# Re-timing the opening of a fused attention and feed-forward kernel, and recutting its last output tile

## The chip, the cores and the metric

One core of one Trainium2 chip. The metric is the device time of one execution in microseconds (us). The kernel before was given as 327.79 us, the median of three executions (327.70 to 327.82). "Span" is the time from the first to the last instruction in a trace; an execution's time is its span plus about 1.8 us.

Engine names as the profile has them: PE is TensorE's products, PEld its weight loads, DVE is VectorE, ACT is ScalarE, POOL is GpSimd, SP is SyncE; a "q" behind a name is the engine's instruction queue, for example where it issues a DMA.

## The reference

Two stages in a row (shortened). Linear attention with cosine weights, for 8 batches, 8 heads, 576 positions and head dimension 64:

```python
def phi(x, c, s):
    r = np.maximum(x, 0.0)
    return np.concatenate([r * c, r * s], axis=-1)
q_p, k_p = phi(q, cos_w, sin_w), phi(k, cos_w, sin_w)
kv  = np.einsum('bhsf,bhsd->bhfd', k_p, v)
z   = np.sum(k_p, axis=2)
num = np.einsum('bhsf,bhfd->bhsd', q_p, kv)
den = np.einsum('bhsf,bhf->bhs', q_p, z)[..., None] + 1e-06
out = num / den
```

then, on 4608 tokens of width 512, RMS normalisation and a gated feed-forward layer of width 1536:

```python
xn = x / np.sqrt(np.mean(x * x, axis=-1, keepdims=True) + 1e-06) * rms_g
g = xn @ w_gate
return (g / (1 + np.exp(-g))) * (xn @ w_val) @ w_out
```

## The kernel before

After an opening of about 31 us the kernel is a long row of products with 512 columns: for each of nine blocks of tokens, 12 steps of gate and value products (`gval_mm`), then output products. Every engine's order is fixed by the program. The opening is where batch 0 is loaded, its attention computed, and the first half of block 0's feed-forward run in small pieces. The parts that the argument touches (cuts marked `...`; V, A, G are VectorE, ScalarE, GpSimd):

```python
load_kv("k", 0, *LOW); load_kv("k", 0, *HIGH)
load_q_tokens(0, 0, 2)
first_v = load_kv("v", 0, *LOW)             # head pairs 0 and 1
load_kv("v", 0, 2, 3); load_kv("v", 0, 3, 4)  # pair 2, pair 3
...
filler(12, idle)          # products on zeros, to get TensorE's clock granted
paced(7, 1); paced(0, 3)
nc.tensor.matmul(psG[0][:, :], lhsT=ones[:, :], rhs=g_row[:, :], start=True, stop=True)
paced(5, 3)
...                       # weight slices are released by first_v
v_cast(A, 0, 0, 1); v_cast(V, 0, 1, 2); v_cast(A, 0, 2, 3)
q_tr_evac(V, 0, 0, psV[0][:, :])
kvz_mm(0, low_banks, LOW)                   # phi(k)' [v, 1], pairs 0 and 1
kvz_copy(A, 0, 0, low_banks[0], LOW); kvz_copy(A, 0, 1, low_banks[1], LOW)
v_cast(V, 0, 3, 4)
kvz_mm(0, high_banks, (2, 3))               # pair 2
filler(1, idle)
nd_half(0, 0, 0, psV[0]); nd_post_half(0, 0, 0, psV[0])   # first half of x tile 0
kvz_mm(0, high_banks, (3, 4))               # pair 3
...
nd_half(0, 0, 1, psO[1]); nd_post_half(0, 0, 1, psO[1])
...
x_sq(0, 0)                                  # ACT square and sum, POOL power
...
x_norm(0, 0)                                # DVE
x_tr_pe(0, 0, psG[1][:, :]); x_tr_evac(V, 0, 0, psG[1][:, :])   # x transposed by TensorE
...
open_ffn(2, (4, 5), 0, 256, parts=(0,))     # gate products of steps 4 and 5
x_tr_pe(0, 2, psA[:, 0, :])                 # transposes of x tile 2
...
# batch 1: k waits for the fourth pair of weight slices
d = load_kv("k", 1)
tc.add_manual_dep(d.ins, weight_dmas[7].ins.name, SYNC_DEP, reason="after the weights")
...
# last output tile, in two halves of 256 columns
for half, bank in ((0, psC[1]), (1, psG[0])):
    c = slice(256 * half, 256 * half + 256)
    for n in range(NNT):
        nc.tensor.matmul(bank[:, 0:256], lhsT=hTs[8][:, n, 3 * P : 4 * P], rhs=wo[:, n, c], ...)
    copy(A, osb[:, c], bank[:, 0:256])
    for i in range(2):
        r0 = (6 + i) * S + 512
        (nc.sync if i == 0 else A).dma_start(
            out=out[r0 : r0 + 64, c], in_=osb[64 * i : 64 * i + 64, c])
```

## Time and profile before

| reading | value | view |
|---|---|---|
| time of the profiled execution, its span | 328.54, 326.73 us | times, page |
| PE busy | 98% of the span | page |
| landing of v: first two pairs, last pair | 10.58, 12.18 us | chain, queue |
| x_norm of tile 0 starts | 16.63 us | chain |
| first full-width gate product (step 6) | 31.43 us | PE timeline |
| end of the last product to end of span | 3.72 us | PE timeline |

The profiled execution took 328.54 us, 0.75 more than the three timed ones.

From the page of the kernel before: the span, each engine's busy time, and the shares of the chain of waits.

```profile
span 326.7 us, 6408 instructions
...
PE 318.9 (98%) x2427; PEld 161.3 (49%) x2427; DVE 186.3 (57%) x412; ACT 175.7 (54%) x365; POOL 31.9 (10%) x67
...
PE 91%; DMA 3%; DVE 2%; ACT 2%; issue 1%; SPq 0%; POOL 0%; DVEq 0%
```

PE is the limit almost everywhere, so a change elsewhere can pay only in PE's few holes or at the two ends.

The chain of waits of the kernel before in the opening (start us, length us, what):

```profile
2.27 8.31 DMA rv<-in_v_dram
...
14.29 0.17 DVE rec L344
...
15.22 0.73 ACT scr L374 x2
...
16.63 0.76 DVE xn L386
17.39 0.05 issue
17.44 0.40 PE psG L411 x4
```

The whole opening hangs on one DMA: v lands at 2.27 + 8.31 = 10.58 us.

VectorE's timeline of the kernel before between the casts of v and the two half normalisations (start us, length us, engine, line, operation, out<-in, shapes, count, and in brackets the idle time before it and what ended it):

```profile
12.20 0.76 DVE L264 CAST vvm<-rv 128x576 bf16<-128x576 f32 x1 [0.24 <-DMA rv<-in_v_dram]
13.06 0.16 DVE L344 TENSOR_SCALAR rec<-psV 128x4 f32<-128x4 f32 x1
...
14.29 0.16 DVE L344 TENSOR_SCALAR rec<-psO 128x4 f32<-128x4 f32 x1 [0.40 <-PE psO L325]
```

The weight loads' timeline of the kernel before, at the transposes of x (L411) and one more hole:

```profile
17.43 0.23 PEld L411 LDWEIGHTS <-xn 128*128 128x128 bf16 x4 [1.20 <-DVE xn L386]
...
19.46 0.23 PEld L411 LDWEIGHTS <-xn 128*128 128x128 bf16 x4 [0.21 <-DVE xn L386]
...
24.45 0.23 PEld L411 LDWEIGHTS <-xn 128*128 128x128 bf16 x4 [0.42 <-DVE xn L386]
...
27.05 0.21 PEld L561 LDWEIGHTS <-wg 128*128 128x128 bf16 x3 [0.26 <-issue]
```

These brackets are the holes that the second part of the change aims at.

ScalarE's timeline of the kernel before in the tail:

```profile
321.73 0.37 ACT L262 COPY osb<-psC 128x256 f32<-128x256 f32 x1 [0.72 <-PE psC L823]
322.14 0.58 ACTq L830 DMA_DIRECT2D out_dram<-osb  x1
323.04 0.37 ACT L262 COPY osb<-psG 128x256 f32<-128x256 f32 x1 [0.94 <-PE psG L823]
323.45 0.50 ACTq L830 DMA_DIRECT2D out_dram<-osb  x1
```

The first store's issue is over (322.72) before the last copy is due (323.04).

### The profile page before, as it was taken

What the parts mean: (1) busy time and instruction counts of PE and PEld (TensorE: products, weight loads), DVE (VectorE), ACT (ScalarE), POOL (GpSimd) and SP (SyncE); (2) the same over time, 40 slices, a digit from 0 to 9 for tenths busy, and PEclk for the clock granted to TensorE, in tenths of its full rate; (3) what the DMA queues carried; (4) which work ended last, traced back from release to release, by engine and by line L of the source; (5) the groups of instructions that cost most, each with busy time, mean ns of one, the idle gap of its engine ahead of it and who ended that gap; (6) DMA issues with size and microseconds to landing.
All of it is one profiled execution on the core that took longest, in us unless ns stands there. A gap on an engine that the chain in (4) does not pass through costs nothing.

```text
span 326.7 us, 6408 instructions
## 1 busy us (share of the span) xinstructions
PE 318.9 (98%) x2427; PEld 161.3 (49%) x2427; DVE 186.3 (57%) x412; ACT 175.7 (54%) x365; POOL 31.9 (10%) x67
## 2 busy tenths in 40 slices
PE   7989999999999999999999999999999999999995
PEld 2578465654445444544454445444544444444443
DVE  6776668777755876578257745773577134203410
ACT  6764775875666457645654576456644233223321
POOL 1660112001100110011001100110011000000000
PEclk9999999999999999999999999999999999999999
DMA  7999999989968967996597569957621400030014
GB/s 258 229 187 228 371 170 334 314 184 185 253 197 177 211 173 171 244 180 166 179 231 186 150 186 229 195 165 208 131 52 32 130 32 0 13 116 2 0 34 96
DMA packets 80193, 53.91 MB, mean 165 GB/s; under 512 B 51361, under 2 KB 67489, under 8 KB 80162
## 3 DMA queue, kind: packets, MB, share of 16 engines
q1 hardware_dynamic: 73120, 48.64, 58.1%
q0 software_dynamic: 6880, 4.72, 10.0%
q8 instruction: 19, 0.31, 0.4%
q10 hardware_dynamic: 162, 0.13, 0.2%
q14 instruction: 12, 0.10, 0.1%
HBM read 37.75 MB, written 9.44 MB: 144 GB/s over the span
## 4 chain that ended last, share of the span: by engine, by line
PE 91%; DMA 3%; DVE 2%; ACT 2%; issue 1%; SPq 0%; POOL 0%; DVEq 0%
PE psG L425 26%; PE psC L445 26%; PE psV L425 26%; PE psA L281 3%; DMA rv<-in_v_dram 3%; PE psA L309 2%; PE psG L445 1%; PE psG L561 1%; PE psO L561 1%; PE psV L561 1%; ACT kpm L208 1%; PE psV L253 1%; ACT sg L434 0%; PE psA L316 0%; DVE xn L386 0%
## 5 line engine op out<-in xcount | busy, mean ns | idle before, releaser
L440 DVE TENSOR_TENSOR hT<-psV,sg 128x512 bf16<-128x512 f32 x102 | 70.3, 690 | 96.3 <-PE psV L425 84.9
L434 ACT ACTIVATE sg<-psG 128x512 f32<-128x512 f32 x102 | 60.5, 593 | 65.6 <-PE psG L425 65.6
L425 PE MATMUL psG<-xnT,wg 128*128 128x512 bf16 (+1 forms) x368 | 92.9, 375 | 0.1
L425 PE MATMUL psV<-xnT,wv 128*128 128x512 bf16 (+1 forms) x368 | 92.7, 374 | 0.0
L445 PE MATMUL psC<-wo,hT 128*128 128x512 bf16 x396 | 89.6, 379 | 0.0
L425 PEld LDWEIGHTS <-wv 128*128 128x128 bf16 x416 | 40.6, 98 | 47.4
L445 PEld LDWEIGHTS <-hT 128*128 128x128 bf16 x420 | 40.2, 98 | 46.4
L425 PEld LDWEIGHTS <-wg 128*128 128x128 bf16 x416 | 38.5, 98 | 41.3 <-DVE xnT L264 0.4
L262 ACT COPY osb<-psC 128x512 f32<-128x512 f32 (+1 forms) x33 | 19.1, 578 | 40.4 <-PE psC L445 39.6
L379 POOL TENSOR_TENSOR rs<-ms,mhalf 128x1 f32<-128x1 f32 x36 | 19.8, 550 | 201.4 <-ACT scr L374 201.4
L386 DVE SCALAR_TENSOR_TENSOR xn<-xt,rs,gb 128x512 bf16<-128x512 f32 x36 | 26.8, 746 | 14.7 <-POOL rs L379 14.7
L374 ACT ACTIVATE scr<-xt 128x513 bf16<-128x513 f32 x36 | 22.9, 635 | 22.4 <-DVE xt L363 22.0
L208 ACT ACTIVATE kpm<-rk,tab 128x256 bf16<-128x256 f32 (+1 forms) x78 | 31.8, 477 | 1.7 <-DMA rk<-in_k_dram 1.7
L363 DVE TENSOR_TENSOR xt<-psA,rec 128x512 f32<-128x512 f32 x35 | 24.2, 692 | 1.2
L210 DVE TENSOR_SCALAR kpm<-rk,tab 128x256 bf16<-128x256 f32 (+1 forms) x84 | 22.2, 331 | 2.2 <-DMA rk<-in_k_dram 2.2
L208 ACT ACTIVATE qp<-rq,tab 128x512 bf16<-128x512 f32 x31 | 21.8, 712 | 0.1
L210 DVE TENSOR_SCALAR qp<-rq,tab 128x512 bf16<-128x512 f32 x33 | 15.4, 480 | 0.3 <-DMA rq<-in_q_dram 0.3
L309 PEld LDWEIGHTS <-qpT 128*128 128x128 bf16 x248 | 11.7, 98 | 6.7 <-issue 0.3
L309 PE MATMUL psA<-kvzs,qpT 128*128 128x65 bf16 x248 | 12.8, 194 | 0.3
L425 PE MATMUL psV<-xnt_tail,wv 128*128 128x512 bf16 x48 | 12.3, 379 | 0.0
L425 PE MATMUL psG<-xnt_tail,wg 128*128 128x512 bf16 x48 | 12.3, 379 | 0.0
L281 PEld LDWEIGHTS <-kpm 64*128 64x128 bf16 x576 | 9.9, 95 | 3.8 <-issue 2.7
(89 smaller groups left out, 167.3 us busy)
## 6 DMA issues: line engine op xcount, KB each, us to landing
out_dram<-osb SPq DMA_DIRECT2D x32, 256.0 KB, 2.6
rv<-in_v_dram SPq DMA_DIRECT2D x22, 288.0 KB, 3.3
rk<-in_k_dram SPq DMA_DIRECT2D x20, 288.0 KB, 3.5
rq<-in_q_dram SPq DMA_DIRECT2D x20, 256.0 KB, 3.2
rk<-in_k_dram SPq DMA_DIRECT2D x2, 1152.0 KB
rq<-in_q_dram SPq DMA_DIRECT2D x2, 1024.0 KB, 10.8
rv<-in_v_dram SPq DMA_DIRECT2D x3, 576.0 KB, 9.3
wo<-in_moe_w_out_dram POOLq DMA_DIRECT2D x4, 384.0 KB, 7.2
```

Source lines behind the costliest of these rows:

```text
L208: nc.scalar.activation(out=out_ap, in_=in_ap, func=AF.Relu, scale=scale)
L210: eng.tensor_scalar(out=out_ap, in0=in_ap, scalar1=scale, scalar2=0.0, op0=ALU.mult, op1=ALU.max)
L281: nc.tensor.matmul(banks[c][:, r * E : (r + 1) * E], lhsT=kp_main[b][lo : lo + 64, j, r, :], rhs=vvm[b % 2][lo : lo + 64, r, j, :], start= ...
L309: nc.tensor.matmul(o[:, g, i, :], lhsT=qpT[(b, 0)][:, h, j * P : (j + 1) * P], rhs=kvz_of(b, h), start=True, stop=True,)
L363: nc.vector.tensor_tensor(out=xt[:, 0:DM].rearrange("p (b h d) -> p b h d", b=2, d=D), in0=o[:, :, :, 0:D], in1=rec[:, :, :].unsqueeze(3). ...
L374: nc.scalar.activation(out=scr[:, :], in_=xt[:, 0 : DM + 1], func=AF.Square, scale=1.0 / math.sqrt(DM), accum_out=ms[:, :],)
L379: nc.gpsimd.tensor_tensor(out=rs[:, :], in0=ms[:, :], in1=mhalf[:, :], op=ALU.pow)
L386: nc.vector.scalar_tensor_tensor(out=xn[:, :], in0=x_of[(b, j)][:, 0:DM], scalar=rs_of[(b, j)][:, :], in1=gb[:, :], op0=ALU.mult, op1=ALU. ...
L425: nc.tensor.matmul(pst[bank][:, cols[0] : cols[1]], lhsT=w[:, t, n * P : (n + 1) * P], rhs=x[:, t, cols[0] : cols[1]], start=(t == 0), sto ...
L434: nc.scalar.activation(out=sg[:, :], in_=psG[bank][:, :], func=AF.Silu)
L440: nc.vector.tensor_tensor(out=hTs[blk][:, n, :], in0=psV[bank][:, :], in1=sg[:, :], op=ALU.mult)
L445: nc.tensor.matmul(bank, lhsT=hTs[blk][:, n, j * P : (j + 1) * P], rhs=wo[:, n, :], start=(n == 0), stop=(n == NNT - 1),)
```

## The change

Its intent: in the opening, let v's casts follow the order of landing and share the last one between two engines; take the gb copy out of ScalarE's later queue; put x_norm of tile 1 earlier, and transposes of x inside groups of products so that PE has other work while it would wait; and make the last output copy and stores small. Core of the diff (cuts marked):

```diff
-    def v_cast(eng, b, r0=0, r1=4):
+    def v_cast(eng, b, r0=0, r1=4, j0=0, j1=NJ):
 ...
+    copy(A, gb[:, :], psG[0][:, :])
     v_cast(A, 0, 0, 1)
 ...
     kvz_mm(0, low_banks, LOW)
-    kvz_copy(A, 0, 0, low_banks[0], LOW)
-    kvz_copy(A, 0, 1, low_banks[1], LOW)
-    v_cast(V, 0, 3, 4)
+    v_cast(V, 0, 3, 4, 0, 5)
+    v_cast(A, 0, 3, 4, 5, NJ)
+    kvz_copy(V, 0, 0, low_banks[0], LOW)
+    kvz_copy(V, 0, 1, low_banks[1], LOW)
     kvz_mm(0, high_banks, (2, 3))
     filler(1, idle)
+    kvz_mm(0, high_banks, (3, 4))
+    q_tr_evac(A, 0, 1, psO[0][:, :], (0, 4))
     nd_half(0, 0, 0, psV[0])
     nd_post_half(0, 0, 0, psV[0])
-    kvz_mm(0, high_banks, (3, 4))
-    q_tr_evac(A, 0, 1, psO[0][:, :], (0, 4))
     kvz_copy(A, 0, 0, high_banks[0], HIGH)
     kvz_copy(A, 0, 1, high_banks[1], HIGH)
-    filler(1, idle)
 ...
-    copy(A, gb[:, :], psG[0][:, :])
 ...
+    x_norm(0, 1)
     q_phi(V, 0, 3, 0)
-    x_norm(0, 1)
-    open_ffn(0, (0, 1), 0, 128)
+    open_ffn(0, (0,), 0, 128)
     x_tr_pe(0, 1, psV[1][:, :])
     x_tr_evac(V, 0, 1, psV[1][:, :])
+    open_ffn(0, (1,), 0, 128, first=1)
 ...
-    open_ffn(2, (4, 5), 0, 256, parts=(0,))
+    open_ffn(2, (4,), 0, 256, parts=(0,))
     x_tr_pe(0, 2, psA[:, 0, :])
     x_tr_evac(A, 0, 2, psA[:, 0, :])
+    open_ffn(2, (5,), 0, 256, first=1, parts=(0,))
     x_norm(0, 3)
+    open_h(1, 2, 0)
 ...
-    open_h(1, 2, 0)
     open_h(2, 4, 0)
+    open_ffn(1, (2, 3), 256, 384)
     open_ffn(0, (0, 1), 384, 512)
     open_h(0, 0, 1)
-    open_ffn(1, (2, 3), 256, 512)
+    open_ffn(1, (2, 3), 384, 512)
 ...
-    for half, bank in ((0, psC[1]), (1, psG[0])):
-        c = slice(256 * half, 256 * half + 256)
+    for (c0, c1), bank in (((0, 384), psC[1]), ((384, 512), psG[0])):
 ...
-        copy(A, osb[:, c], bank[:, 0:256])
+        copy(A, osb[:, c0:c1], bank[:, 0 : c1 - c0])
```

More of the change, by code (lines that the diff above doesn't have):

```diff
@@ L264, in copy @@
             eng.tensor_copy(out=o, in_=i)
-    def v_cast(eng, b, r0=0, r1=4):
+    def v_cast(eng, b, r0=0, r1=4, j0=0, j1=NJ):
         copy(
-            eng, vvm[b % 2][:, r0:r1, :, 0:D],
-            raw[("v", b)][:, r0:r1, :].rearrange("p r (j d) -> p r j d", d=D),
+            eng, vvm[b % 2][:, r0:r1, j0:j1, 0:D],
+            raw[("v", b)][:, r0:r1, j0 * D : j1 * D].rearrange("p r (j d) -> p r j d", d=D),
         )
@@ L542 @@
     nd_post(0, 1, psA)
-    q_phi(A, 0, 2, 1)
     x_sq(0, 1)
@@ L546 @@
     gval_slice(1152, 1536)
+    q_phi(A, 0, 2, 1)
     filler(9, psV[1][:, :])
@@ L550, with open_ffn @@
     q_phi(A, 0, 3, 1)
-    def open_ffn(pair, steps, c0, c1, base=0, parts=(0, 1)):
+    def open_ffn(pair, steps, c0, c1, first=0, parts=(0, 1)):
         x = xnT[0]
@@ L558, in open_ffn @@
                 bank = pairs[pair][a]
-                lo = base + 256 * i + c0 % 256
+                lo = 256 * (first + i) + c0 % 256
                 for t in range(NDT):
@@ L595 @@
     open_ffn(0, (0, 1), 128, 256)
-    open_ffn(1, (2, 3), 0, 256, parts=(0,))
+    open_ffn(1, (2,), 0, 256, parts=(0,))
     nd_pe(0, 3, psA)
     nd_post(0, 3, psA)
+    open_ffn(1, (3,), 0, 256, first=1, parts=(0,))
     x_norm(0, 2)
@@ L819 @@
     osb = four.tile([P, DM], FP32, name="osb", tag="osb")
-    for half, bank in ((0, psC[1]), (1, psG[0])):
-        c = slice(256 * half, 256 * half + 256)
+    for (c0, c1), bank in (((0, 384), psC[1]), ((384, 512), psG[0])):
         for n in range(NNT):
             nc.tensor.matmul(
-                bank[:, 0:256], lhsT=hTs[8][:, n, 3 * P : 4 * P], rhs=wo[:, n, c],
+                bank[:, 0 : c1 - c0], lhsT=hTs[8][:, n, 3 * P : 4 * P], rhs=wo[:, n, c0:c1],
                 start=(n == 0), stop=(n == NNT - 1),
             )
-        copy(A, osb[:, c], bank[:, 0:256])
+        copy(A, osb[:, c0:c1], bank[:, 0 : c1 - c0])
         for i in range(2):
@@ L830 @@
             (nc.sync if i == 0 else A).dma_start(
-                out=out[r0 : r0 + 64, c], in_=osb[64 * i : 64 * i + 64, c]
+                out=out[r0 : r0 + 64, c0:c1], in_=osb[64 * i : 64 * i + 64, c0:c1]
             )
```

## The prediction

> **What bounds the kernel.** TensorE. The page gives PE 98% busy of a 326.7 us span at full granted clock, and 91% of the chain of waits is PE. So only three things can move: the opening's chain up to about 27 us, the few PE holes in it, and the tail after the last product. The steady state (about 295 us) has the same instructions in the same order on every engine.
>
> **Opening, before.** The chain of waits: v pairs land at 10.58, 11.36 and 12.18; the last pair's cast on VectorE takes 0.75 (12.20 to 12.95); products of pair 3, eviction, second half product (13.83), normalise (14.29 to 15.13), x_norm 16.63, transposes of x 17.44. Then PE loses about 0.2 before x tile 1 (19.46), about 0.3 before tile 2 (24.45, both waiting for xn) and about 0.3 at 27.05 (for tile 3's eviction): about 0.8 in all.
>
> **The change there.**
> - Split last cast: estimate 0.49 on VectorE (320 elements) beside 0.40 on ScalarE (256), from 0.75 and 0.67 for 576. The Trainium skill, "VectorE: DVE Perf Modes", section "Mode 2×_2P", says that a copy whose outermost dimension is odd but equal on both sides may run two elements a cycle. The trace disagrees: one pair (9 x 64) takes 0.755, as long as two pairs (0.755), so I cost the 5 x 64 part at single rate. Gain about 0.25 on pair 3.
> - Against it: VectorE now also evicts the low half (two of 0.3), and the first half product moves behind pair 3. First normalise starts about 13.45 instead of 13.06, and the second follows it back to back at about 14.2 instead of 14.29. Gain at x_norm only 0.05 to 0.15; the rest of the split is lost in VectorE's queue.
> - gb copy, 0.62, moves into ScalarE's 0.82 wait for v: free, and off the later queue.
> - x_norm(1) ahead of the query scaling: transposes of tile 1 about 0.5 earlier, but half of that product group now stands behind them. Net about 0.1 to 0.2.
> - Transposes of tiles 2 and 3 inside groups: one hole stays partly (xn(2) is ready about 23.85), the one at 27.05 goes, since 0.9 us of other products now covers the eviction. About 0.3.
> PE should reach the first full-width group at about 30.9 instead of 31.43: 0.5 gained (0.2 to 0.8). It should persist: loads land 1 us or more ahead of need.
>
> **Tail.** 384 + 128 columns need the same PE time (1.31 + 1.32). The last copy shrinks from 0.37 to about 0.26 (estimate from 0.58 at 512 and 0.37 at 256). But the first part ends 0.65 later, its copy (about 0.48) ends about 0.2 before the last product, and ScalarE then issues a store (0.57 before) ahead of the last copy in program order. That copy starts about 0.45 late, the last store about 0.3 late. Halving it to 32 KB buys at most 0.1: 64 KB take 2.2 to land, 128 KB 2.3 to 2.4. The Trainium skill, "DMA: Bandwidth & Descriptors", section "Anatomy of one DMA", puts about 2 us fixed; the trace agrees. Tail: about 0.25 lost.
>
> **Predicted:** 327.5 us, 8 in 10 between 327.0 and 327.9. Faster by over 2%: 0.01; within: 0.98; slower: 0.01.
>
> **Right if** the profile shows x_norm(0) at about 16.55, no PE hole at 27, first full-width group near 30.9, the last copy waiting for ScalarE's store issue, and last issue to end unchanged near 3.3 us.
>
> **Wrong if** ScalarE's issue does not hold the copy (then 327.2), if the split runs faster or VectorE's queue hides less (326.9), or if new waits on xn or evictions refill the holes (327.9).

## The result, and the profile after

First comparison: changed 328.04 us (median of six executions, 327.72 to 329.37), before 327.76 us (six, 327.70 to 328.36). The ratio is 1.0015, 95% interval 0.9996 to 1.0035: the same within 2%. Ratios here and below are the mean time of one kernel's fast executions over that of the other's of the same rounds, so not quite the ratio of the medians quoted. 328.04 lies above the predicted 327.0 to 327.9.

The traces seem to contradict this: the span of the changed kernel is 326.24 us, 0.5 shorter than that of the kernel before. From the page of the changed kernel:

```profile
span 326.2 us, 6439 instructions
...
PE 318.8 (98%) x2442; PEld 161.0 (49%) x2442; DVE 186.3 (57%) x414; ACT 175.6 (54%) x364; POOL 32.3 (10%) x67
...
PE 90%; DMA 2%; DVE 2%; ACT 2%; issue 1%; SPq 0%; POOL 0%; ACTq 0%
```

Its chain of waits in the opening:

```profile
2.43 7.85 DMA rv<-in_v_dram
...
13.22 0.17 DVE rec L344
...
14.89 0.73 ACT scr L374 x2
...
16.30 0.76 DVE xn L386
17.06 0.05 issue
17.10 0.40 PE psG L411 x4
```

v landed at 10.28, 0.30 us earlier than in the trace of before, and no part of the change touches that load or anything before it. x_norm is 0.33 earlier, so nearly all of that is the landing. The two traces must therefore be compared from v's landing on, not from time 0.

VectorE's timeline of the changed kernel, same place as before:

```profile
11.82 0.49 DVE L264 CAST vvm<-rv 128x320 bf16<-128x320 f32 x1 [0.17 <-DMA rv<-in_v_dram]
12.22 0.28 DVE L264 CAST kvzs<-psG 128x130 bf16<-128x130 f32 x1
12.42 0.28 DVE L264 CAST kvzs<-psV 128x130 bf16<-128x130 f32 x1
13.22 0.16 DVE L344 TENSOR_SCALAR rec<-psV 128x4 f32<-128x4 f32 x1 [0.52 <-PE psV L325]
...
13.97 0.15 DVE L344 TENSOR_SCALAR rec<-psO 128x4 f32<-128x4 f32 x1
```

The cast fell from 0.76 to 0.49 us. But the first half normalisation now starts 1.40 us after the cast's start (13.22 less 11.82) against 0.86 before, and the second follows it without idle time. The gain has gone.

The weight loads at the transposes of x in the changed kernel:

```profile
17.10 0.23 PEld L411 LDWEIGHTS <-xn 128*128 128x128 bf16 x4 [1.38 <-DVE xn L386]
...
18.68 0.23 PEld L411 LDWEIGHTS <-xn 128*128 128x128 bf16 x4 [0.21 <-DVE xn L386]
...
23.67 0.23 PEld L411 LDWEIGHTS <-xn 128*128 128x128 bf16 x4 [0.41 <-DVE xn L386]
...
25.61 0.27 PEld L411 LDWEIGHTS <-xn 128*128 128x128 bf16 x4
```

The hole that stood at 27.05 has no counterpart. The first full-width gate product starts at 30.76 instead of 31.43, 0.67 earlier, of which 0.34 come after the first transpose (13.66 us against 14.00). From there the two traces run in step to the last product: the offset of 0.67 stays constant.

ScalarE in the tail of the changed kernel:

```profile
321.70 0.48 ACT L262 COPY osb<-psC 128x384 f32<-128x384 f32 x1 [1.36 <-PE psC L826]
322.21 0.55 ACTq L833 DMA_DIRECT2D out_dram<-osb  x1
322.80 0.27 ACT L262 COPY osb<-psG 128x128 f32<-128x128 f32 x1 [0.62 <-PE psG L826]
323.10 0.50 ACTq L833 DMA_DIRECT2D out_dram<-osb  x1
```

The last product ended at 322.33, but its copy starts at 322.80: the engine was issuing the first store until 322.76. The tail grew from 3.72 to 3.90 us.

### The profile page after: what moved, and what is told of

It reads as the page before. It is cut to its first block, busy times and chain, and to the rows that moved or that the text cites. A ratio compares the mean times of both kernels' runs of the same rounds, so it can differ in the third digit from the quotient of the medians.

```text
span 326.2 us, 6439 instructions
## 1 busy us (share of the span) xinstructions
PE 318.8 (98%) x2442; PEld 161.0 (49%) x2442; DVE 186.3 (57%) x414; ACT 175.6 (54%) x364; POOL 32.3 (10%) x67
## 3 DMA queue, kind: packets, MB, share of 16 engines
q0 software_dynamic: 6880, 4.72, 10.0%
## 4 chain that ended last, share of the span: by engine, by line
PE 90%; DMA 2%; DVE 2%; ACT 2%; issue 1%; SPq 0%; POOL 0%; ACTq 0%
PE psG L425 26%; PE psC L445 26%; PE psV L425 26%; PE psA L281 3%; DMA rv<-in_v_dram 2%; PE psA L309 2%; PE psG L445 1%; PE psG L561 1%; PE psO L561 1%; PE psV L561 1%; ACT kpm L208 1%; PE psC L826 1%; PE psV L253 1%; ACT sg L434 0%; PE psA L316 0%
```

## The experiments

Eighteen runs on the chip, in five groups, each group on one chip and sharing executions of the kernel before. A timed comparison of 0.1% is hard here, since executions of one kernel spread over 1.5 us; so each trace was also measured from its own marks. All of them in one table, the marks being: landing of v's first pairs; from the start of VectorE's cast of the last v pair to x_norm of tile 0; from the first transpose of x to the first full-width gate product; ScalarE's wait for k of batch 1; from the start of the opening's last sigmoid to the start of the 36th one after it; and from the end of the last product to the end of the span. "wd" marks traces with a withdrawn clock (below). The texts call the 36th sigmoid the 60th; it is the interval of 36 that gives their figures in the traces.

| trace | v lands | cast to x_norm | transpose to full width | wait for k | 36 sigmoids | tail |
|---|---|---|---|---|---|---|
| before | 10.58 | 4.43 | 14.00 | 0 | 106.06 | 3.72 |
| changed | 10.28 | 4.48 | 13.66 | 0 | 106.06 | 3.90 |
| e1 before again | 9.51 | 4.65 | 14.00 | 0 | 106.06 | 3.74 |
| e2 changed again (wd) | 10.50 | 5.01 | 13.66 | 0.30 | 106.27 | 3.89 |
| e3 tail only | 10.00 | 4.42 | 14.00 | 0.03 | 106.06 | 3.91 |
| e4 opening only | 10.42 | 4.47 | 13.66 | 0.40 | 106.37 | 3.73 |
| e5 k after slice 3 (wd) | 10.23 | 5.49 | 13.66 | 0 | 106.05 | 3.89 |
| e6 k after slice 5 | 10.04 | 4.45 | 13.66 | 2.47 | 108.43 | 3.90 |
| e7 last copy on VectorE | 10.03 | 4.46 | 13.66 | 0 | 106.05 | 3.83 |
| e8 no filler | 10.73 | 4.34 | 13.66 | 0.53 | 106.49 | 3.89 |
| e9 early fillers | 9.89 | 4.83 | 13.66 | 0.09 | 106.06 | 3.92 |
| e10 four together | 10.29 | 4.35 | 13.66 | 0 | 106.06 | 3.73 |
| e11 second half only | 9.66 | 4.50 | 13.66 | 1.26 | 107.39 | 3.91 |
| e12 one store per part | 9.24 | 4.72 | 13.66 | 0 | 106.06 | 9.01 |
| e13 before | 9.59 | 4.47 | 14.00 | 0 | 106.06 | 3.75 |
| e14 changed | 9.71 | 4.53 | 13.66 | 0.47 | 106.44 | 3.90 |
| e15 before | 10.07 | 4.42 | 13.99 | 0 | 106.05 | 3.74 |
| e16 changed | 10.68 | 4.46 | 13.66 | 0 | 106.70 | 3.89 |
| e17 mended version (wd) | 9.80 | 4.84 | 13.66 | 0 | 106.35 | 3.75 |
| e18 mended version | 10.53 | 4.35 | 13.66 | 0 | 106.05 | 3.73 |

### First group: controls, and the two ends apart

**e1_before_again**: no edit, the kernel before.

> The kernel before, unchanged, as a control. The one trace of it came from an execution of 328.54 us, while six timed executions had a median of 327.76, so that trace is about 0.8 us off the typical one. Theory A (the trace of before was a slow execution: its loads landed late at the start): a second trace shows a span near 325.9, v landing at or before 10.28 instead of 10.58, and the first full-width gate product near 31.0 or earlier instead of 31.43. Theory B (the opening is the same every time and the timed executions differ from the profiled one elsewhere): 31.4 again. Ratio to before 1.000 within 0.001.

Measured: 328.53 us (six, 327.67 to 329.55), ratio 1.0019 (1.0000 to 1.0037). v landed at 9.51 and the first full-width product came at 30.58; the span was 325.89. So theory A stands: the first trace of before was a slow draw. But an unchanged copy missed the expected ratio by 0.19%, more than the whole effect under study.

**e2_after_again**: no edit, the changed kernel.

> The changed kernel, unchanged, as a control. Theory A (a real loss of about 0.3 us from the changed tail and an opening that gains nothing over a typical execution of before): ratio 1.0008 to 1.0015, times near 328.0 with few above 328.5. Theory B (the change is neutral or 0.3 us better, and the six first executions drew badly): ratio 0.999 to 1.000. Theory C (the changed opening sometimes lets the TensorE clock be withdrawn, or leaves it withdrawn longer): executions spread from 327.7 to 329.4 again, and the slow ones have a mean clock below 0.998.

Measured: 328.56 us (327.76 to 329.18), ratio 1.0012 (0.9997 to 1.0028). Two of its six executions had a mean granted clock (the share of full speed that TensorE was given) of 0.994, both slow (329.01 and 329.18); so had two of the six of e1 (329.55, 329.04). Theory C is right in that withdrawn clocks exist, and wrong in tying them to the change. The trace of e2 fell on one. TensorE's clock in three stretches of it (columns: stretch, length, PE busy, granted clock, DMA share, GB/s):

```profile
5.80:9.20 3.40, 2.75 (x9) 1.00 1.00 339
9.20:12.60 3.40, 3.40 (x56) 0.50 0.88 271
12.60:16.00 3.40, 2.89 (x64) 0.99 1.32 169
```

For 3.4 us in the middle of the opening TensorE ran at half clock; x_norm came 0.5 us later after the cast than in the other traces.

**e3_tail_only**:

```diff
 # before, with
-    for half, bank in ((0, psC[1]), (1, psG[0])):   # 256 and 256 columns
+    for (c0, c1), bank in (((0, 384), psC[1]), ((384, 512), psG[0])):
```

> Before with only the last tile cut in 384 and 128 columns. From the two traces, end of the last product to end of the span is 3.71 us before and 3.87 after, so plus 0.15 to 0.3 us: ratio 1.0005 to 1.001, and no wider spread than before. If the tail is what made the change slow, this run alone gives the whole plus 0.28.

Measured: 328.10 us (327.77 to 329.39), ratio 1.0006 (0.9991 to 1.0021). The tail is 3.91 against 3.72 to 3.75 in every trace with the old one: a cost of 0.17, seen in each trace with the new cut and nothing else in the tail changed. It is less than 0.28, and the spread is as wide as elsewhere, so the tail alone is not the story.

**e4_open_only**: the changed opening with before's tail (the same lines put back).

> The changed opening with the tail of before. If the opening gains what the traces show beyond the earlier landing of v (0.67 less 0.30), minus 0.4 us: ratio 0.9988. If the opening gains nothing over a typical execution of before: 1.000. If the opening is what spreads the times: executions from 327.4 to 329 here, and tight ones in the run with the tail alone.

Measured: 328.15 us (327.31 to 329.34), ratio 1.0007 (0.9989 to 1.0026). The clock cannot decide between the two values expected. The trace does: the opening is 0.34 shorter, but 0.31 of that is lost again within the 36 sigmoids. ScalarE in that stretch, first in the trace of before, then in e4:

```profile
35.95 0.60 ACT L434 ACTIVATE sg<-psG 128x512 f32<-128x512 f32 x1 [1.13 <-PE psG L425]
36.47 1.70 ACT L208 ACTIVATE kpm<-rk,tab 128x256 bf16<-128x256 f32 x4
```

```profile
35.47 0.60 ACT L434 ACTIVATE sg<-psG 128x512 f32<-128x512 f32 x1 [1.13 <-PE psG L425]
36.47 1.70 ACT L208 ACTIVATE kpm<-rk,tab 128x256 bf16<-128x256 f32 x4 [0.40 <-DMA rk<-in_k_dram]
```

A new wait: ScalarE arrives before k of batch 1 has landed. In the traces of before this instruction came without a wait for that DMA (one of 0.03 us in e3).

I had not looked for the landing itself. The views do not print it, but the semaphore records kept with the traces hold it: 36.44 us in the trace of before and also in e4. With k landed long before (e5, e10, e17, e18 below), the instruction starts 0.49 us after the sigmoid ahead of it. Measured against that, k was between 0.17 us early (e13) and 0.14 late (e3) in the five traces with before's opening. So there was next to nothing in hand even before the change.

### Second group: the wait for k, the tail, the filler

**e5_k_after_slice3** and **e6_k_after_slice5**: release k of batch 1 earlier, or later.

```diff
-    tc.add_manual_dep(d.ins, weight_dmas[7].ins.name, ...)
+    tc.add_manual_dep(d.ins, weight_dmas[5].ins.name, ...)   # e5;  weight_dmas[9] in e6
```

> The changed kernel with the load of k of batch 1 released by the third pair of weight slices instead of the fourth. Theory (part of the opening's gain is given back because k of batch 1 has not landed when ScalarE reaches it, as in two of three traces of the changed opening, 0.3 to 0.4 us of wait and 0.2 to 0.3 us of later products): no wait of ScalarE for k, and from the first full-width gate product to the 60th sigmoid after it the same 106.06 us as in the traces without the wait, in place of 106.27 and 106.37. Rival (the 0.2 to 0.3 us are lost on the engines for another reason): 106.2 or more can come again. Time at most 0.3 us less, within the noise.

> The dose the other way: k of batch 1 released by the fifth and last pair of weight slices, which landed 3.4 to 3.7 us after the fourth. Theory: ScalarE waits for k about 2.5 to 3.7 us longer, and the products after it are late by about 2 to 3.5 us; ratio 1.006 to 1.011. Rival: below 0.5 us.

Measured: e5 328.10 us (four, 327.75 to 329.00), ratio 0.9999 (0.9979 to 1.0019); its trace is a withdrawn-clock one, yet has no wait for k and 106.05 us over the 36 sigmoids. There k landed at 32.97 us, 3.8 before ScalarE took it up at 36.78. e6 330.31 us (two), ratio 1.0062 (1.0041 to 1.0084): a wait of 2.47 us and 108.43, so 2.4 us lost. ScalarE in e5, then in e6:

```profile
36.29 0.60 ACT L434 ACTIVATE sg<-psG 128x512 f32<-128x512 f32 x1 [1.13 <-PE psG L425]
36.78 1.69 ACT L208 ACTIVATE kpm<-rk,tab 128x256 bf16<-128x256 f32 x4
```

```profile
38.13 0.91 ACT L208 ACTIVATE kpm<-rk,tab 128x256 bf16<-128x256 f32 x2 [2.47 <-DMA rk<-in_k_dram]
```

The dose works in both directions, and the loss of PE follows the wait nearly one for one. The give-back is shown: closing PE's holes only lets the engines arrive earlier at a load that is paced by the DMAs. It is a matter of luck in each execution (released as before, k landed 8.4 to 10.0 us after its issue): of the ten traces with the changed second half and k released as before (changed, e2, e4, e7, e8, e9, e11, e12, e14, e16), five waited 0.3 us or more. Against 106.05, those five lost 0.22, 0.32, 0.44, 1.34 and 0.39, so 0.27 on average over the ten. Half of that is the 1.34 of e11, which has another first half. In the seven traces whose opening is exactly the changed one (without e8, e9 and e11), three waited and the average is 0.13. With k released earlier (e5, e10, e17, e18) none of four waited.

**e7_last_copy_vector**:

```diff
-        copy(A, osb[:, c0:c1], bank[:, 0 : c1 - c0])
+        copy(A if c0 == 0 else V, osb[:, c0:c1], bank[:, 0 : c1 - c0])
```

> The changed kernel with the last 128 columns copied by VectorE, which is idle, instead of ScalarE. Theory (ScalarE's issue of the first store, 0.55 us, holds the last copy 0.45 us past the end of the last product): the copy starts within 0.05 of the last product, the last stores are issued about 0.3 us earlier, and last product to end of span is 3.60 us against 3.90 in the changed kernel and 3.73 before. Rival (the tail is longer because of the store's shape, rows of 512 bytes, and not of the hold): 3.85 to 3.9 again.

Measured: 328.33 us (four, 327.69 to 328.91), ratio 1.0008 (0.9990 to 1.0026). The last product ended at 322.08; the copy and the stores on ScalarE's queue:

```profile
321.96 1.38 ACTq L833 DMA_DIRECT2D out_dram<-osb  x2
...
322.12 0.29 DVE L264 COPY osb<-psG 128x128 f32<-128x128 f32 x1 [9.63 <-PE psG L826]
```

The hold is gone (0.04 us instead of 0.47), but the tail is 3.83, not 3.60. The last store is issued 0.24 us earlier after the last product and lands only 0.17 earlier (2.64 us after it against 2.81): it comes 0.1 us behind the first stores' issue, its own issue takes 0.73 instead of 0.50, and it takes longer to land; from its landing to the end of the span there is 0.08 more. So the mechanism is right and its price was mis-sized: taking the hold away gave back 0.07 us, not 0.3.

**e8_no_filler**:

```diff
     kvz_mm(0, high_banks, (2, 3))
-    filler(1, idle)
     kvz_mm(0, high_banks, (3, 4))
```

> The changed kernel without the filler product between pair 2 and pair 3. In its trace the last pair's casts end at 12.31 and the products of pair 3 start at 12.49, behind the filler (12.17). Theory (the split cast is worth nothing because pair 3 waits for the filler and then VectorE's two normalisations run back to back behind the first half product): x_norm of tile 0 comes 0.12 us earlier, 5.90 us after v's landing against 6.02 to 6.06 in the changed and 6.00 to 6.05 in the kernel before. Rival (VectorE's low evictions hold the first half product): no change, 6.0. A clock withdrawn during the opening would spoil this reading: then look at the clock records.

Measured: 329.10 us (four, 327.57 to 329.50), ratio 1.0017 (0.9989 to 1.0045). x_norm came 5.89 us after v's landing: 5.90 had been expected. Then the trace waits 0.53 us for k and loses 0.44, more than the filler's removal had gained. The theory holds, and so does the give-back.

### Third group

**e9_early_fillers**:

```diff
-    filler(12, idle)
+    filler(16, idle)
     paced(7, 1)
+    filler(1, idle)
 ...
     paced(5, 3)
+    filler(1, idle)
```

> The changed kernel with six more filler products in the first 10 us (four before the first paced product, one after it, one after the last), where TensorE stood idle 0.7 to 1.5 us. In the two traces where the clock was withdrawn (9.2 to 12.6 us), the full-clock window before it began at 5.8 us and held about 0.65 to 0.9 us of idling and 1.0 us of the one-partition product. Theory (executions near 329 are those whose clock is withdrawn at 9.2 us after a half idle window): none of six executions has a mean clock of 0.993 or 0.994, and none with a full clock record is above 328.6. In the kernels so far 8 of 46 executions of new kernels had such a clock. Rival (the withdrawal has nothing to do with that idling): one or two of six again, and times up to 329.4. The fillers stand in idle time, so x_norm of tile 0 stays 6.0 us after v's landing.

(The count in it was slightly off: it was 9 of 44 executions.) Measured: 328.71 us (six, 328.31 to 329.34), ratio 1.0019 (1.0000 to 1.0038). No clock of 0.994 in six, but three executions of 329.06 to 329.34 with a full clock record, which the theory excluded. And the fillers did not stay in idle time: in the trace the clock was granted late (7.2 us), the transposes of q, behind a longer row of half-speed products, came 0.9 us later than in the first trace of changed (10.50 against 9.56), and x_norm came 6.70 us after v. A failed mend. Whether the fillers prevent withdrawal stays open: six executions without one are too few, and the next kernel with fillers (e10) had none either.

**e10_four_together**: e8's edit, e5's edit, e9's fillers, and before's tail.

> The version that the runs point to: the changed opening without the filler before pair 3, k of batch 1 released by the third pair of slices, the six early fillers, and the tail of before. Theory: x_norm 5.90 after v's landing, 13.66 from the first transpose of x to the first full-width group, 106.05 to the 60th sigmoid, tail 3.73; span less v's landing 315.67 against 316.15 before and 315.9 to 316.0 changed; ratio to before 0.9985, and no execution near 329. Rival (noise of landing and clock covers it all): ratio within 0.9995 to 1.001.

Measured: 327.78 us (six, 327.62 to 328.95), ratio 0.9993 (0.9975 to 1.0011). One execution near 329, against the expectation. In the trace every mark but one came as expected; the last v pair landed 1.66 us behind the first in place of 1.5 to 1.6, so x_norm was 6.03 after v. Inconclusive by the clock, as expected by the marks.

**e11_second_half_only**: the changed kernel, with everything ahead of x_norm of tile 0 put back.

```diff
-    v_cast(V, 0, 3, 4, 0, 5)
-    v_cast(A, 0, 3, 4, 5, NJ)
-    kvz_copy(V, 0, 0, low_banks[0], LOW)
-    kvz_copy(V, 0, 1, low_banks[1], LOW)
+    kvz_copy(A, 0, 0, low_banks[0], LOW)
+    kvz_copy(A, 0, 1, low_banks[1], LOW)
+    v_cast(V, 0, 3, 4)
 ...   # and the order of the first half product, the gb copy and x_sq as before
```

> The changed kernel with everything ahead of x_norm of tile 0 put back as before (whole cast of the last v pair, low evictions by ScalarE, first half product before pair 3, gb copy late), keeping the transposes of x inside the groups and the reordered sigmoids. Theory (the first half of the opening's change is worth nothing): x_norm of tile 0 at 6.00 to 6.05 after v, first full-width gate product 20.48 to 20.53 after v, as in the changed kernel. Rival (the split is worth 0.1 or more and hid in the noise): 0.1 or more later than that.

Measured: 328.82 us (four, 328.03 to 328.86), ratio 1.0011 (0.9991 to 1.0031). x_norm 6.07 after v, first full-width product 20.53 after v: within 0.02 of the expected ranges. The split cast with all that goes with it is worth nothing. This trace has the longest wait for k, 1.26 us.

**e12_one_store_per_part**:

```diff
-        for i in range(2):
-            r0 = (6 + i) * S + 512
-            (nc.sync if i == 0 else A).dma_start(
-                out=out[r0 : r0 + 64, c0:c1], in_=osb[64 * i : 64 * i + 64, c0:c1])
+        (nc.sync if c0 == 0 else A).dma_start(
+            out=out.rearrange("(b s) m -> b s m", s=S)[6:8, 512:576, c0:c1], in_=osb[:, c0:c1])
```

> The changed kernel with one store for each part of the last tile: 384 columns from SyncE, 128 columns from ScalarE, instead of two stores each. Theory (the tail is last issue plus a landing that grows with stores close ahead of it): the last copy starts within 0.05 of the last product, the only last store is issued about 0.33 after it against 0.76 in the changed kernel, and last product to end of span is 3.55 to 3.7. Rival (ScalarE is held by something other than its own issue of a store): the copy starts 0.4 late again and the tail is 3.85.

Measured: 333.02 us (four, 332.52 to 333.66), ratio 1.0146 (1.0125 to 1.0167). The last copy did start at once, 0.04 us after the last product (321.73), with ScalarE free:

```profile
321.77 0.27 ACT L262 COPY osb<-psG 128x128 f32<-128x128 f32 x1 [0.19 <-PE psG L826]
322.06 0.64 ACTq L831 DMA_DIRECT2D out_dram<-osb  x1
```

So the hold is ScalarE's own issue of a store, and the rival falls. But the tail is 9.0 us: the merged stores landed only at 328.7 and 329.8 us, and from 324 to 328 us they moved 41 GB/s. The Trainium skill, "DMA: Bandwidth & Descriptors", section "Rules for kernel authors", says that the number of DMA engines is set by the access patterns' slowest dimension, so that an outermost dimension of 2, as this store has in memory, leaves at most two of sixteen. The trace agrees: from 324 to 328 us the busy share of the 16 engines was 0.12, worth 1.9 of them. It does not show the engines singly.

### Fourth group: two unchanged copies of each kernel, side by side

**e13_before_control**, **e15_before_control2** (before), **e14_changed_control**, **e16_changed_control2** (changed): no edits.

> The kernel before, unchanged, as a new kernel. Hypothesis S (a kernel in the place of the new one reads slower than the kernel before in its own place, whatever its code; nine of ten new kernels but those with a known cost read 1.000 to 1.002): ratio 1.001 to 1.002 again, with executions near 329. Hypothesis N (that was chance): 0.999 to 1.001.

> The changed kernel, unchanged, in the same place. By the traces' sum (x_norm plus 0.05, holes minus 0.34, tail plus 0.17, and 0 to 1.3 us of waiting for k of batch 1) the mean should be within 0.3 us of that of the kernel before in the same place (0.1 us less without the wait for k, 0.2 us more with 0.3 us of it). If the change itself costs what the first executions showed (0.28 us in the median), it is 0.28 above e13 and e15 here.

> As e13: the kernel before, unchanged, once more, so that twelve executions of each of the two kernels stand in the same place on one chip.

> As e14: the changed kernel, unchanged, once more. In all four traces: opening from the first transpose of x to the first full-width group 14.00 before and 13.66 changed; tail 3.72 to 3.74 and 3.89 to 3.91; if a trace falls on an execution near 329 with a full clock record, its clock record should start later than 9 us (TensorE released late), and if it starts before 7.3 us that explanation falls.

Measured: before 328.49 and 327.89 us (ratios 1.0005, 0.9972 to 1.0037, and 0.9986, 0.9957 to 1.0016); changed 328.37 and 329.01 (ratios 1.0000, 0.9970 to 1.0030, and 1.0019, 0.9983 to 1.0055). The suspicion that the place of a new kernel reads slow (hypothesis S) finds no support, though intervals of 0.3% either way could not exclude 0.1%. The mean of the changed copies (328.45 and 329.10) lies above that of before's (328.44 and 328.01), the second pulled up by one execution of 331.05 with a clock of 0.990.

The trace of e16 caught an execution of 329.04 with a full clock record. Its clock was granted at 6.56 us, so the explanation by a late grant falls. What it has is a late v (10.68) and this, at the start of a block in mid-kernel (PE's timeline):

```profile
126.30 1.04 PE L425 MATMUL psG<-xnT,wg 128*128 128x512 bf16 x4 [0.47 <-DMA xnT<-xn]
```

A DMA transpose of x landed 6.0 us after its issue, where the same one in the changed kernel's first trace took 2.6; everything after runs 0.64 us later. The same wait stands in e17's trace, where it cost 0.29. It lies far from anything that the change touches. Two of the fifteen traces with the changed second half have such a wait and none of the five without, which is too few to say that the change has no part in it.

### Fifth group: the mended version

**e17_opening_k_old_tail** and **e18_same_again**: the changed kernel with e8's edit (no filler), e5's edit (k released by the third pair of slices) and before's tail; one kernel, twice.

> As e10 but without the early fillers (which delayed x_norm in e9): the changed opening without the filler before pair 3, k of batch 1 released by the third pair of slices, the tail of before. Theory: x_norm 4.36 after the landing of v's last pair (4.45 before), 13.66 to the first full-width group, 106.05 to the 60th sigmoid, tail 3.73: the span less v's landing 315.7 against 316.1 to 316.2 before, so a mean over the executions about 0.4 us below that of the kernel before in the same call, ratio 0.9985 to 0.999, with withdrawn clocks as often as before. Rival (it only trades one wait for another): ratio 1.000 or above, and a new wait in the trace.

> The same kernel as e17 once more, for twelve executions of it against eleven of before on one chip: as e17.

Measured: 327.79 us (six, 327.60 to 329.26), ratio 0.9986 (0.9970 to 1.0003), and 327.80 (five, 327.49 to 328.24), ratio 0.9990 (0.9974 to 1.0006). Both agree with the expected 0.9985 to 0.999. The mean of the eleven executions is 327.93, that of the kernel before in the same call 328.25, so 0.32 with an error of about 0.23. Part of that is the draw of withdrawn clocks (one of eleven against two of nine); without those executions it is 327.80 against 328.04, 0.24. The marks of e18 are those expected, and its span less v's landing is 315.73 against 316.15 in the first trace of before; e17's trace was a withdrawn-clock one. Each interval still touches 1, so "0.1% better than before" is likely and not proven by the clock alone.

## Why the prediction was right or wrong

It was wrong: 328.04 against 327.0 to 327.9, and slower where faster was forecast. Point by point.

**The range, and the noise in it.** The prediction took 327.79 with its spread of 0.12 us as the kernel's time. Over all groups the kernel before has 73 executions from 327.46 to 330.86, median 328.11, and 46 of the 73 are above 327.9. The changed kernel has 24, mean 328.60 (standard error 0.16), against 328.23 (0.07). So 0.37 us, with an error of about 0.18. The range of 0.9 us holds only 27 of the 73 executions of the unchanged kernel. What spreads the executions, as far as the traces show: v's landing (9.24 to 10.73 us), a withdrawn clock (6 of the 24, and 11 of the 67 of before with a clock record; the three traces that show one have x_norm 0.5 to 1.0 us later after the cast), the wait for k, and late DMA transposes (0.29 and 0.64). Executions that no trace caught may have other causes. The profiled execution of the changed kernel itself, 328.01 us, had no wait for k. Its span less v's landing (315.96) is below those of before (316.09 to 316.38), so the forecast of a small gain held in it, and what put it above the range is that v landed at 10.28; in the 327.53 us execution of before (e13) v landed at 9.59. That the median fell outside a range so narrow is in part luck.

**"It should persist: loads land 1 us or more ahead of need."** This is the step of the mechanism that failed. The page gave no landing for k of batch 1 and I passed over it; the only sign was that ScalarE had not waited. In place of 1 us in hand, k came between 0.17 us early and 0.14 late in the five traces with before's opening. After the opening was shortened, three of the seven traces with exactly that opening wait 0.30 to 0.47 us for it, and of 0.34 gained 0.13 are given back on average (0.27 over all ten traces with the changed second half). e5 and e6 show it by dose.

**Opening, the split cast: "Gain at x_norm only 0.05 to 0.15".** Measured from the cast's start, 4.43 before and 4.48 changed: minus 0.05 to 0, and e11 agrees. The prediction had the mechanism, VectorE's queue and the first half product behind pair 3, but overlooked that the filler stood in front of pair 3's products: e8, without it, gains 0.1.

**The cast's rate** was right: 0.49 estimated for 320 elements, 0.49 measured. The reason first given for it was not: it took these casts to contradict the Trainium skill, "VectorE: DVE Perf Modes", section "Mode 2×_2P", which asks of a copy between two places in SBUF that the outermost dimension be even, or odd and equal on both sides, for two elements a cycle. The operand records kept with the trace show one run of 576 elements read and 9 x 64 written: odd on one side and not equal. Two pairs are 1152 read and 18 x 64 written, both even, and took the same 0.755 us. So the trace agrees with the page.

**Holes: "About 0.3" for tiles 2 and 3, "0.1 to 0.2" for tile 1.** Together 0.34 were gained after the first transpose in every trace with the second half of the change. The hole at 27.05 goes, as predicted; the one before tile 2 stays whole (0.42 and 0.41) where "partly" was written. The sum "0.5 gained" was too large by about 0.2, through the split and tile 1.

**gb copy: free.** It ran from 9.41 to 9.98, ahead of v at 10.28. Right.

**Tail: "about 0.25 lost".** 0.17 in every trace. The hold was predicted at 0.45 and measured at 0.47; e12 proves its cause. The mis-sized terms: the store with half the bytes lands sooner, so last issue to end of span fell from 3.28 to 3.14 where "unchanged near 3.3" was written. Most of a store's landing did not depend on its size: 2.0 us for 32 KB, 2.2 for 64 KB, 2.3 for 128 KB. The Trainium skill, "DMA: Bandwidth & Descriptors", section "Anatomy of one DMA — SWDGE (gpsimd) path", gives its fixed 2 us for DMAs that GpSimd issues; these stores were issued by ScalarE and SyncE.

**The sum.** Split 0.05 lost, holes 0.34 gained, tail 0.17 lost, waiting for k 0.13 lost on average (0.27 over the ten traces): 0.01 to 0.15 us slower. The executions say 0.37 with an error of 0.18; leaving out those with a clock of 0.995 or less, 328.32 (18 executions) against 328.05 (62, with six that have no clock record), 0.27. The sum and the times agree only within about two standard errors. Whether a remainder of 0.1 to 0.35 us is real, and what it is, stays open. That the sum's causes are the main ones is supported, not proven, by the mended version, which comes out 0.3 below before with an error of 0.2.

## What to carry to other kernels

Before forecasting a gain of 0.1%, submit an unchanged copy and look at its spread: here a copy of the same kernel read 0.19% slow, and two traces could be compared only from the landing of the load that starts the chain. When you close holes on the bounding engine, ask of every load whose landing you cannot see how much it has in hand; no wait in the trace is not slack. In a tail, look at which engine must issue a store before its last copy, and keep the outermost dimension of a store wide.

## What the Trainium skill lacked or had wrong

- "TensorE: Matmul & The Clock Gate", Part 1, "What's actually happening": the table there gives the half clock after one or more idle windows of about 3.4 us. The length agrees (3.41 us at half clock in e2, e5 and e17). But in e2 the 3.4 us before the withdrawal had PE busy for 2.75 (81%), while in the first trace of before the same stretch, busy for 2.42, was followed by full clock. In all three traces the full clock had been granted at 5.78 to 5.86 us, and in none of the other seventeen in that interval; the page gives no threshold by which to tell them apart.
- "DMA: Bandwidth & Descriptors", section "Rules for kernel authors": it advises one transfer of 128 partitions instead of two to disjoint halves. Where the two halves go to two distant blocks of rows, so that memory's outermost dimension is 2, following it took the tail from 3.9 to 9.0 us (e12). The row on using all 16 engines explains it; the two rows do not refer to each other.
- The same page, section "Issuing engines are not separate DMA queues", calls the time that a sequencer needs to start a DMA usually small beside the DMA itself. In this tail it was not: 0.55 us of issue on ScalarE, beside 2.0 us for the last store to land, held a copy for 0.47 us after its product was ready.
- No page that I found gives the spread of a DMA transpose's landing: 2.6 us and 6.0 us for the same one in two executions.
